# A new order of entries for the first two groups, and unused products at the end removed, in a blocked linear attention that feeds a leaky-ReLU MLP

## The chip, the cores and the metric

The kernel runs on one core of one Trainium2 chip. The metric is the device time of one execution in microseconds (us), as the median of several runs. The profile shows one execution of the program, taken by the hardware profiler; its times count from the span's start.

The engines are named as the profile names them: PE (TensorE, matrix products) with PEld (its weight loads), DVE (VectorE), ACT (ScalarE), POOL (GpSimd) and SP (SyncE, which issues the transfers). Each executes its own instructions, and semaphores order them across engines.

## The reference

Everything is float32 to the caller except the two weight matrices, which arrive as float64. The first part is lightning attention over blocks of 64 tokens with a running state, the second a two-layer MLP on the same 3072 tokens.

```python
B, H, S, D = 4, 8, 768, 64            # q, k, v; lam has one decay for each head
for b in range(S // 64):
    sl = slice(b * 64, (b + 1) * 64)
    intra = einsum('bhic,bhjc->bhij', qb, kb) * Dmask     # Dmask = lam ** (i - j), lower triangle
    intra = einsum('bhij,bhjd->bhid', intra, vb)
    inter = einsum('bhid,bhde->bhie', qb * lam_pow, kv_state)
    out[:, :, sl] = intra + inter
    kv_state = lam ** 64 * kv_state + einsum('bhsd,bhse->bhde', kb * rev_pow, vb)

x = out.transpose(0, 2, 1, 3).reshape(3072, 512)
h = x @ w_in                          # 512 x 2048
g = maximum(0.01 * h, h)
return g @ w_out                      # 2048 x 512
```

## The kernel before

**Tiling.** The tokens are 24 chunks of 128, six for each batch. Four chunks are a group of 512 tokens (`GC = 4`), so there are six groups, numbered 0 to 5. The hidden width of 2048 is cut into eight pieces of 256, p = 0 to 7, called weights here.

**Three products for one.** Each operand of a product is split into a high part `h`, a low part `l` and their mixture `m`, and each product is done three times, with `h`, `l` and `m`. So each weight has tiles `wh`, `wl`, `wm`, and the attention's output has `xh`, `xl`, `xm`.

**Attention of one chunk.** `load_kq` and `load_v` issue the transfers (L338, L388). `transposes` turns k and q on TensorE (L403), k into a bank of PSUM, q into `pt`. ScalarE copies both out (L414, L415). L419 scales k by the decay, and L423 scales q. `scores` makes the products of k and q, and of k and v, in `psc`; both use the helper at L313. VectorE masks the first (L452) and adds the second to the state (L457, L459); GpSimd decays the state (L462). `outputs` makes the output in `po`, also at L313, in three parts. Between the second and the third stands a tiny copy, `seen_po` (L491), on VectorE or ScalarE. ScalarE then writes `xh` (L507), and VectorE `xl` (L508) and `xm` (L510).

**Weights.** `w_in(p)` loads a weight in two halves as raw 64-bit words (L566) into one of three buffers, `raw0` to `raw2`, in turn. Each half is turned into float32 by three instructions on ScalarE (L578, L580, L582) and two on VectorE (L584, L585). Then `parts` makes `wh` on ScalarE (L591) or VectorE (L593), and `wl` (L596) and `wm` (L602) on VectorE.

**Units.** `up(g, p)` is the product of one group with one weight: 24 matmuls of 512 columns (two blocks of 128 of the weight's 256 columns; in each, four pieces of the depth for `h`, for `l` and for `m`). A block lies in one of three banks (`b10`, `b11`, `b2`). After `h` and `l` ScalarE scales the bank (L658); then `m` is added, ScalarE applies the leaky ReLU (L661), and the result is stored to DRAM (L664). `up` can also be given some of the group's four chunks: `("up", 1, 1, 0, 3)` is group 1, weight 1, chunks 0 to 2 of the group, with matmuls of 384 columns, and `("up", 1, 1, 3, 4)` the last chunk, with matmuls of 128. When all groups are through, `down` multiplies by `w_out` (L700), and each result is combined (L722, L729) and stored (L732).

**Order.** Nothing is issued as it is written. The entries of the list `seq` are turned into operations, each with an engine, a planned length and what it needs. `Plan.emit` gives every operation a planned start and emits all in that order, so each engine executes its instructions in the plan's order. In `seq`, `("a", c)` is a whole chunk alone, `("b", 4)` starts chunks 4 and 5, `("r", c)` is a round (the outputs of chunk c with the scores of chunk c+1 and the transposes of chunk c+2), `("wi", p)` loads and splits a weight, `("ls",)` and `("lt",)` load keys and queries in small blocks that are turned by VectorE (L374, L383). Behind the list, the entries for groups 2 to 5 and for `down` are appended by a loop.

**Fillers.** Where the plan's second pass expects TensorE to wait over 0.4 us, and until the bank `b10` has its first use, `plan.idle` puts in transposes of the identity that nothing reads, one for each 0.22 us. They are L266, `busy`. Eleven stand ahead of everything (`WARM`).

**Constants of the order.** `KT` names the bank for the k transposes of chunks 0 to 3, and `EARLY` the number of blocks for which that bank is left out of the turn. For chunks below `QS`, L423 is done by VectorE straight from `pt`, otherwise by GpSimd from ScalarE's copy. For chunks below `KM` the plan may give L419 to VectorE, otherwise it is GpSimd's. For chunks below `GOFIRST`, the products of k and q come ahead of those of k and v.

**The end.** Behind `plan.emit()` stand matmuls whose result nobody reads: 12 with half of the rows and 12 with a quarter (L802), and 8 of 64 columns (L809).

## Time and profile before

| | |
|---|---|
| three runs | 610.75, 611.75, 612.11 us; median 611.75 |
| span of the profiled execution | 610.3 us |
| mean granted clock of TensorE | 0.997 |
| products of units (L640), in all | 392 for each of `h`, `l`, `m`; 376 of them 512 columns wide, 8 of 384, 8 of 128 |
| fillers (L266) | 30 |
| first product of a unit | 30.41 us |
| transfers in the first 20 us | DMA engines 96% busy, 205 GB/s |
| L566, from issue to landing | 4.1 / 5.5 / 7.3 us (shortest, median, longest) |
| DVE and ACT from 40 to 60 us | 19.3 and 17.1 of 20 us busy |

A row of the profile's timeline has the start, the length, the engine, the line, what it writes and reads, the shape and the number of instructions in it. In brackets stands the idle time of the engine ahead of the row and what ended it. The lengths of TensorE's rows overlap: matmuls are pipelined, and one of 512 columns is listed with 0.39 us though the next starts 0.23 us later. So what a matmul costs is read from start to start.

### The profile page before, as it was taken

What the parts mean: (1) busy time and instruction counts of PE and PEld (TensorE: products, weight loads), DVE (VectorE), ACT (ScalarE), POOL (GpSimd) and SP (SyncE); (2) the same over time, 40 slices, a digit from 0 to 9 for tenths busy, and PEclk for the clock granted to TensorE, in tenths of its full rate; (3) what the DMA queues carried; (4) which work ended last, traced back from release to release, by engine and by line L of the source; (5) the groups of instructions that cost most, each with busy time, mean ns of one, the idle gap of its engine ahead of it and who ended that gap; (6) DMA issues with size and microseconds to landing.
All of it is one profiled execution on the core that took longest, in us unless ns stands there. A gap on an engine that the chain in (4) does not pass through costs nothing.

```text
span 610.3 us, 13012 instructions
## 1 busy us (share of the span) xinstructions
PE 601.9 (99%) x5426; PEld 497.6 (82%) x5426; DVE 313.2 (51%) x418; ACT 269.9 (44%) x430; POOL 86.6 (14%) x90
## 2 busy tenths in 40 slices
PE   7799999999999999999999999999999999999999
PEld 5688888888888878888788888888888888888887
DVE  5899764334243426326366755545454544636531
ACT  4678974444455646555577522222222313214111
POOL 2564412114133004104000000000000000000000
PEclk9899999999999999999999999999999999999999
DMA  9999775666889878886686843524333343333201
GB/s 201 236 261 263 215 204 126 175 154 176 192 212 245 212 222 219 212 242 212 233 302 219 278 155 103 173 69 139 137 104 134 111 136 111 132 104 126 82 1 69
DMA packets 147754, 105.18 MB, mean 172 GB/s; under 512 B 123632, under 2 KB 124400, under 8 KB 147696
## 3 DMA queue, kind: packets, MB, share of 16 engines
q1 hardware_dynamic: 147552, 104.36, 58.8%
q8 instruction: 42, 0.69, 0.5%
q14 instruction: 16, 0.13, 0.1%
q10 hardware_dynamic: 144, 0.00, 0.0%
HBM read 68.69 MB, written 35.65 MB: 171 GB/s over the span
## 4 chain that ended last, share of the span: by engine, by line
PE 95%; DMA 2%; ACT 1%; DVE 1%; issue 0%; SPq 0%; ACTq 0%
PE b L640 42%; PE b L700 18%; PE po L700 11%; PE psc L700 11%; PE po L313 4%; PE psc L313 4%; PE pt L700 4%; DMA g<-gs 1%; DMA att<-in_v_dram 1%; PE pt L403 1%; DMA att<-in_q_dram 1%; PE po L403 0%; PE psc L802 0%; ACT att L415 0%; PE b L266 0%
## 5 line engine op out<-in xcount | busy, mean ns | idle before, releaser
L682 ACT ACTIVATE xh<-att 128x1024 fp32r<-128x1024 f32 x48 | 50.8, 1060 | 149.1 <-PE b L700 133.6
L683 DVE SCALAR_TENSOR_TENSOR xl<-att,xh 128x1024 fp32r<-128x1024 f32 x48 | 58.7, 1223 | 97.5 <-ACT xh L682 97.5
L640 PE MATMUL b<-xm,wm 128*128 128x512 f32 (+2 forms) x392 | 104.5, 392 | 0.7 <-ACT b L658 0.7
L640 PE MATMUL b<-xh,wh 128*128 128x512 f32 (+2 forms) x392 | 103.2, 386 | 0.8 <-ACT xh L507 0.8
L640 PE MATMUL b<-xl,wl 128*128 128x512 f32 (+2 forms) x392 | 103.4, 387 | 0.0
L640 PEld LDWEIGHTS b<-xh,wh 128*128 128x128 f32 x392 | 72.9, 188 | 16.0 <-ACT xh L507 0.9
L640 PEld LDWEIGHTS b<-xl,wl 128*128 128x128 f32 x392 | 72.7, 188 | 15.1 <-DVE wl L596 0.3
L640 PEld LDWEIGHTS b<-xm,wm 128*128 128x128 f32 x392 | 71.4, 188 | 16.0 <-ACT b L658 1.1
L658 ACT ACTIVATE b<-b 128x512 f32<-128x512 f32 (+2 forms) x97 | 56.1, 580 | 60.6 <-PE b L640 60.5
L661 ACT ACTIVATE gs<-b 128x512 f32<-128x512 f32 (+2 forms) x97 | 57.0, 592 | 44.2 <-PE b L640 38.3
L700 PE MATMUL b<-wh,xh 128*128 128x512 f32 x192 | 74.7, 389 | 0.0
L700 PE MATMUL b<-wl,xl 128*128 128x512 f32 x192 | 74.7, 389 | 0.0
L685 DVE SCALAR_TENSOR_TENSOR xm<-xl,xh 128x1024 fp32r<-128x1024 f32 x48 | 58.7, 1225 | 4.7
L462 POOL TENSOR_TENSOR att<-att 128x256 f32<-128x256 f32 x40 | 34.4, 861 | 58.7 <-DVE att L459 58.7
L700 PEld LDWEIGHTS b<-wh,xh 128*128 128x128 f32 x192 | 36.1, 188 | 7.5
L700 PEld LDWEIGHTS b<-wl,xl 128*128 128x128 f32 x192 | 36.0, 188 | 7.5
L423 POOL TENSOR_TENSOR att<-att 128x512 f32<-128x512 f32 (+1 forms) x20 | 25.3, 1265 | 95.6 <-PE po L313 34.7
L452 DVE TENSOR_TENSOR att<-psc,att 128x512 f32<-128x512 f32 x24 | 16.5, 689 | 43.1 <-PE psc L313 43.1
L584 DVE TENSOR_SCALAR w<-w 128x512 int32<-128x512 int32 x32 | 19.6, 612 | 36.0 <-ACT w L578 35.9
L700 PE MATMUL psc<-wh,xh 128*128 128x512 f32 x96 | 37.3, 389 | 0.0
L700 PE MATMUL psc<-wl,xl 128*128 128x512 f32 x96 | 37.3, 389 | 0.0
L700 PE MATMUL psc<-wm,xm 128*128 128x512 f32 x96 | 37.3, 389 | 0.0
(79 smaller groups left out, 810.4 us busy)
## 6 DMA issues: line engine op xcount, KB each, us to landing
att<-g SPq DMA_DIRECT2D x48, 512.0 KB, 3.3
g<-gs SPq DMA_DIRECT2D x47, 512.0 KB, 4.0
raw<-in_moe_w_in_dram SPq DMA_DIRECT2D x16, 512.0 KB, 5.5
raw<-in_moe_w_out_dram SPq DMA_DIRECT2D x16, 512.0 KB, 4.8
att<-in_k_dram SPq DMA_DIRECT2D x48, 128.0 KB, 4.3
att<-in_v_dram SPq DMA_DIRECT2D x24, 256.0 KB, 4.5
out_dram<-gs SPq DMA_DIRECT2D x23, 256.0 KB, 2.1
wo<-w SPq DMA_DIRECT2D x8, 512.0 KB, 5.9
```

Source lines behind the costliest of these rows:

```text
L313: nc.tensor.matmul(dst[HALF[cols]], lhsT=lhsT[HALF[rows]], rhs=rhs[HALF[rows]], start=start, stop=True, skip_group_check=True)
L423: add(eng, us, lambda: e.tensor_tensor(o, x, _bc(pow_q, 2, 2)[:, :, m, :], op=ALU.mult), ["fq", dep], [f"qsT{i}"])
L452: add("DVE", 0.69, lambda: nc.vector.tensor_tensor(sc, psc[:, :, lower, :], decay, op=ALU.mult), ["psc", "fk"], ["sc"])
L462: add("POOL", 0.7, lambda new=new, j=j: nc.gpsimd.tensor_tensor(state[(j + 1) % 4], new, _bc(lam_c, 2, D), op=ALU.mult), [f"st{j % 4}", "f ...
L584: add("DVE", 0.42, lambda: nc.vector.tensor_scalar(d, d, 3, None, op0=ALU.logical_shift_left), [], [key])
L640: nc.tensor.matmul(dst, lhsT=w[z][:, kk * 2 * P + f * P:kk * 2 * P + (f + 1) * P], rhs=x[z][:, kk, toks], start=start and kk == 0, stop=kk ...
L658: add("ACT", ns, lambda b=b: nc.scalar.activation(out=b, in_=b, func=AF.Copy, bias=0.0, scale=S + 1.0), [], [kb], rank=-1.5)
L661: add("ACT", ns, lambda b=b, r=r: nc.scalar.activation(out=r, in_=b, func=AF.Prelu, bias=0.0, scale=1.0 / WS, alpha=0.01), [kb], [f"gs{jg} ...
L682: add("ACT", 1.05, lambda: nc.scalar.activation(out=h, in_=graw[j], func=AF.Copy, bias=0.0, scale=NEAR), reads, wr("h"))
L683: add("DVE", 1.25, lambda: nc.vector.scalar_tensor_tensor(l, graw[j], 1.0, h.bitcast(F32), op0=ALU.mult, op1=ALU.subtract), reads + [f"rh{ ...
L685: add("DVE", 1.25, lambda: nc.vector.scalar_tensor_tensor(m, l.bitcast(F32), -S, h.bitcast(F32), op0=ALU.mult, op1=ALU.add), [f"rh{j}", f" ...
L700: nc.tensor.matmul(acc[tb][z // 2][:, cols], lhsT=ring[j][z][:, f * T + tb * P:f * T + (tb + 1) * P], rhs=W[pp][z][:, f * d_model:(f + 1) ...
```

## The change

The list for the first two groups is another one. No unit is split in it any more, and weight 1 is loaded behind chunk 1 rather than behind chunk 3. Five constants differ. The products behind `plan.emit()` are gone.

```diff
-    KT, EARLY = "b11", 2
-    QS = 4
-    KM = 2
+    KT, EARLY = "b11", 1
+    QS = 6
+    KM = 0
...
-    GOFIRST = 3
+    GOFIRST = 2
...
-    seq = [("a", 0), ("a", 1), ("a", 2), ("a", 3), ("wi", 1), ("b", 4), ("r", 4), ("up", 0, 1), ("wi", 0), ("r", 5),
-           ("wi", 2), ("wi", 3), ("up", 0, 0), ("up", 0, 2), ("up", 0, 3), ("r", 6), ("up", 1, 1, 0, 3), ("r", 7),
-           ("wi", 4), ("up", 0, 4), ("wi", 7), ("up", 1, 1, 3, 4), ("up", 1, 3), ("up", 0, 7), ("up", 1, 2),
-           ("wi", 6), ("up", 0, 6), ("wi", 5), ("ls",), ("up", 0, 5), ("r", 8), ("lt",), ("up", 1, 7), ("r", 9),
-           ("up", 1, 4), ("r", 10), ("up", 1, 0), ("r", 11), ("up", 1, 6), ("up", 1, 5)]
+    seq = [("a", 0), ("a", 1), ("wi", 1), ("a", 2), ("a", 3), ("wi", 0), ("b", 4), ("r", 4), ("wi", 4), ("up", 0, 1),
+           ("wi", 2), ("up", 0, 0), ("up", 0, 4), ("r", 5), ("r", 6), ("wi", 3), ("wi", 7), ("up", 0, 2),
+           ("up", 0, 3), ("wi", 6), ("r", 7), ("wi", 5), ("up", 0, 7), ("up", 1, 0), ("up", 1, 7), ("up", 1, 4),
+           ("up", 1, 5), ("up", 1, 6), ("up", 0, 6), ("ls",), ("lt",), ("up", 1, 2), ("up", 0, 5), ("r", 8),
+           ("r", 9), ("r", 10), ("up", 1, 3), ("up", 1, 1), ("r", 11)]
...
     plan.emit()
-
-    a, b = ring[0][0], W[0][0]
-    spare = acc[0] + acc[1]
-
-    def strips(n, times):
-        k = P // n
-        for _ in range(times):
-            for i in range(n):
-                r = slice(i * k, (i + 1) * k)
-                nc.tensor.matmul(spare[i], lhsT=a[r, 0:P], rhs=b[r, 0:T], start=True, stop=True, skip_group_check=True)
-
-    strips(2, 6)
-    strips(4, 3)
-    f = graw[0]
-    for _ in range(4):
-        for i in range(2):
-            nc.tensor.matmul(spare[2][HALF[i], 0:C2], lhsT=f[:, 0:C2], rhs=f[:, 0:C2], start=True, stop=True, skip_group_check=True)
```

In the built program this moves instructions on every engine up to the end of group 1; behind that, the order on TensorE is the same up to the removed products. TensorE has 1152 unit matmuls, all 512 columns wide, and 51 fillers; fourteen of them stand between the k and the q transposes of chunk 3. Ahead of the first product of a unit TensorE does the same scores and outputs, and the transposes of one half chunk fewer (q of chunk 5).

SP's order at the start is: k, q, v of chunk 0, k, q, v of chunk 1, both halves of weight 1, k, q, v of chunk 2, q and k of chunk 3, a half of weight 0, v of chunk 3, the other half of weight 0, k and q of chunk 4, both halves of weight 4, v of chunk 4. Before, it was: chunks 0 and 1, a half of weight 1, q and k of chunk 2, the other half of weight 1, v of chunk 2, q and k of chunk 3, q of chunk 4, v of chunk 3, a half of weight 0, k of chunk 4, q of chunk 5, v of chunk 4, the other half of weight 0.

ACT's order from the copy of chunk 3's k to the first product is now: L580 L578 L582 of weight 0's first half, L578 of its second half, L415 of chunk 3, L580 and L582 of the second half, L507 of chunk 2, L580 of weight 4, L415 of chunk 4, L582 of weight 4, L491 and L507 of chunk 3. Before, it was: L491, L507 of chunk 2, L415, L591 of weight 1, L580 and L582 of weight 0's first half, L491, L415, L507 of chunk 3, and only then L578 for both halves.

DVE's order there is now: L508 and L510 of chunk 1, L596 and L602 of weight 1, L423 and L452 of chunk 2, L459, L423 of chunk 3, L584 of weight 0, L491, L459, L585, L584, L508 of chunk 2, L452 of chunk 3.

## The prediction

> **What bounds the kernel now.** I read the page first. Its busy row and its chain of waits agree: TensorE works 99% of the span, and the end is a chain of its products.

> ```profile
> span 610.3 us, 13012 instructions
> PE 601.9 (99%) x5426; PEld 497.6 (82%) x5426; DVE 313.2 (51%) x418; ACT 269.9 (44%) x430; POOL 86.6 (14%) x90
> PEclk9899999999999999999999999999999999999999
> ```

> So time is only won where TensorE idles, runs at a lower clock, or does work that can go. The list of who TensorE waited for puts the longest waits at the start: 1.8 us for the values of chunk 3, 1.6 for VectorE's L459, 1.4 for the identity. Second view, TensorE in order of time before the first product of a unit (columns: start, length, what ran, and idle time before it):

> ```profile
> 24.43 1.57 PE L313 MATMUL psc<-att 64*64 64x64 f32 x64 [1.79 <-DMA att<-in_v_dram]
> 27.19 1.46 PE L313 MATMUL po<-att 64*64 64x64 f32 x48
> 28.58 0.66 PE L403 MATMUL pt<-att 128*128 128x128 f32 x4
> 29.16 0.46 PE L313 MATMUL po<-att 64*64 64x64 f32 x16
> 30.41 0.97 PE L640 MATMUL b<-xh,wh 128*128 128x512 f32 x3 [0.78 <-ACT xh L507]
> ```

> The first product starts at 30.41. From there on TensorE's idle time is one wait of 0.68 us at 224. So **the time is the moment of the first product, plus a fixed amount of product work, plus the tail**. Third, the clock, in stretches of 3.4 us (columns: stretch, length, busy time of each engine, granted clock, DMA share, GB/s):

> ```profile
> 21.57:24.98 3.41, 1.60 (x58) 1.32 (x60) 2.34 (x4) 2.20 (x3) 3.41 (x4) 1.00 1.02 279
> 24.98:28.40 3.42, 3.42 (x92) 2.97 (x87) 2.35 (x4) 1.41 (x2) 1.04 (x2) 0.50 0.80 178
> 28.40:31.80 3.40, 2.62 (x42) 2.02 (x35) 3.37 (x5) 2.69 (x6) 1.87 (x1) 1.00 1.04 266
> ```

> After a stretch with 1.60 of 3.41 us busy (47%) the next ran at half clock; after 2.62 of 3.40 it did not. Fourth, ScalarE before the first product:

> ```profile
> 25.84 0.79 ACT L580 ACTIVATE low<-raw 128x512 uint16<-128x512 uint32 x1 [1.45 <-DMA raw<-in_moe_w_in_dram]
> 28.72 0.16 ACT L491 COPY att<-po 128x2 f32<-128x2 f32 x1 [1.47 <-PE po L313]
> 29.27 0.59 ACT L415 COPY att<-pt 128x512 f32<-128x512 f32 x1 [0.39 <-PE pt L403]
> 29.75 0.60 ACT L507 ACTIVATE xh<-po 128x512 fp32r<-128x512 f32 x1
> ```

> ScalarE keeps its written order: at 25.84 it had stood 1.45 us for a weight. The conversions of the second half of weight 0 start at 30.24, behind the L507 of chunk 3, which releases the first product.

> **The change, part by part.** *The first product.* In the changed order SyncE issues raw, raw (weight 1) ahead of chunk 2; then k2, q2, v2, q3, k3, raw, v3, raw (weight 0), k4, q4, raw (weight 4). The set issued ahead of the third raw is the one issued before 17.96 in the old trace, so I start there, with the old slots:

> ```profile
> 17.96 1.01 SPq L338 DMA_DIRECT2D att<-in_q_dram  x2
> 19.07 0.46 SPq L388 DMA_DIRECT2D att<-in_v_dram  x1
> 19.58 0.73 SPq L566 DMA_DIRECT2D raw<-in_moe_w_in_dram  x1
> 20.41 0.96 SPq L338 DMA_DIRECT2D att<-in_k_dram  x2
> 21.46 2.32 SPq L338 DMA_DIRECT2D att<-in_q_dram  x2
> ```

> Raw 0.73, v3 0.46, raw 0.73, k4 0.96, q4 2.32 and some 0.08 between issues: v3 goes out at 18.8 (19.07 before), the second raw at 19.3, weight 4's first half at 23.5. L566's own view gives 4.1, 5.5 and 7.3 us to landing (min, median, max), so weight 4 lands at 29.0 (27.6 to 30.8), weight 0 at 24.8.

> That matters because of ScalarE's new order: L578 of weight 0, L415 of q3, L580, L582, L507 of chunk 2, **L580 of weight 4**, L415 of q4, L582, L491 and L507 of chunk 3. Two weights now stand ahead of what releases the first product. Queued behind that L580 is L491, for which TensorE's last part of chunk 3's output waits. From 29.0: L580 0.65 to the next start (13.23 to 13.88 in the old trace), L415 0.48 (29.27 to 29.75), L582 0.65: L491 at 30.8. From L491 to the first product took 30.41 - 28.72 = 1.69; chunk 5's q transposes (0.28 of them after L491's end) and their copy (0.15 of delay to L507) move away: 1.26. **First product at 32.0, so +1.6.** The second weight gives a floor: 24.8, plus 0.59, 0.48, 0.65, 0.65, 0.6 on ScalarE, 0.7 and 0.7 on VectorE (L508, L452) and 0.93 for the output products puts L491 at 30.1 anyway. With both landings at their minimum I get 30.6 (+0.2), with weight 4 at its maximum 33.8 (+3.4).

> *The clock.* In the last 4.5 us before 32.0 TensorE has the output products of chunk 3 (0.93 and 0.46) and nine fillers of L266, 0.11 each (the q transposes of the same shape take 0.66 for four with 0.33 of latency in it): 2.4 of 4.5, or 1.8 of 3.41. That lies between 1.60 (throttled) and 2.62 (not), nearer the first. I take a throttled stretch; all in products it costs half of 3.42, 1.7; some of it falls in the wait: **+1.2** (0 to 1.7).

> [...]

> *The moved transposes.* Chunk 5's q transposes now stand behind the first product: **+0.44**, four starts 0.11 apart (up to the row's 0.66).

> *Whole units.* Group 1's unit of weight 1 goes from 24 products of 384 columns and 24 of 128 to 24 of 512. TensorE's starts:

> ```profile
> 64.38 0.86 PE L640 MATMUL b<-xh,wh 128*128 128x384 f32 x4
> 65.08 0.85 PE L640 MATMUL b<-xl,wl 128*128 128x384 f32 x4
> ...
> 78.07 0.56 PE L640 MATMUL b<-xh,wh 128*128 128x128 f32 x4
> 78.47 0.61 PE L640 MATMUL b<-xl,wl 128*128 128x128 f32 x4
> ```

> Four of 384 take 0.69 from start to start, four of 128 take 0.40 to 0.44, and four of 512 take 0.91 (93.08 to 93.98 in the same view): 6 x 0.69 + 6 x 0.42 - 6 x 0.91 = 1.2. **-1.2**, all on TensorE's path.

> *The tail.* The last store is issued at 607.26 and lands 1.7 later (the median of L732's two half stores), at 609.0. The unused products run on until 609.39 and the program's end waits for them. Out: **-0.4** (0 if the end waits for something else, -0.45 at most).

> *Costed at nothing.* Fillers rise from 30 to 51; fourteen stand ahead of q3's transposes, which wait for `pt` anyway until VectorE's L423 of chunk 2, now behind both L596 and L602 of weight 1 (1.6 and 1.2 us). If that wait is gone they cost 14 x 0.11 = 1.5. Chunk 0's key scaling goes from VectorE (0.67) to GpSimd (1.06), idle for 8.07 us there; the q scalings of chunks 4 and 5 go from GpSimd (1.27, 1.93) to VectorE (0.69 each), covered because weight 1's and half of weight 0's parts are now made before the first product; uncovered, 1.4. Chunk 2's score order (keys by values first) waits for v2, in the same place in the data. The wait of 0.68 at 224 may go or double. Rounds 9 to 12 stand four or five groups of four products apart (0.91 each): the closest pair in the old order, 140.28 and 147.07, cost no idle time.

> Sum: +1.6 + 1.2 + 0.44 - 1.2 - 0.4 = **+1.6 us**. The profiled execution's 610.3 becomes 611.9; the median of the three runs, 611.75, lies 1.45 above its span, so the forecast is **613.4**.

> **The rivals.**
> 1. *The delay without the throttled stretch*: 1.6 - 1.2 = +0.4, 612.2. For it: more fillers, and 1.8 us is not 1.6. Against it: the wait is longer than the old one.
> 2. *The weights are in time* (the other side). If weight 0 lands by 23.2 and weight 4 by 25, ScalarE stands nowhere and values of chunk 3 set the start: 24.1 (0.3 sooner), then the old 6.0 to the first product, less 0.9 (products of 1.57 and 1.46 at the half clock take 1.16 and 0.93 elsewhere) and 0.43: 28.8 or so, -1.6. Sum -1.6 + 0.44 - 1.2 - 0.4 = -2.8, 609.0. It decides from a first product at 30.4 without a throttled stretch. For it: two weights of the old order landed 1.5 us apart. Against it: the median of 5.5 us.
> 3. *Weight 4 lands at its latest*: first product at 33.8, sum +3.4, 615.2. For it: one raw issue alone held SyncE for 2.70 us.
> 4. *The list starves products later*: weights 4, 7 and 5 are asked for sooner than in the old order. Against it: some 5 us of VectorE's work on weights 1 and 0 (L596, L602, L584, L585) is done before the first product instead of behind it. A starved unit would cost what rival 3 costs, and counts into its chance.

> **How the numbers follow.** This kernel can tell 0.2%, 1.2 us, from no change: 610.5 to 613.0. Forecast 0.47, rival 1 0.23, rival 2 0.15, rival 3 0.15. Rival 2 is faster; rival 1 is no change, with a little of the forecast (0.02); the rest is slower: 0.15, 0.25, 0.60. The range leaves out most of rival 2 and the far end of rival 3: 610.9 to 616.0; the forecast's own is 612.4 to 614.4.

> **What would show it.** Right: L580 or L578 idle for a weight of `moe_w_in` just ahead of L507 of chunk 2 or 3; a first L640 near 32; a stretch at 0.50 around it; no products of 384 or 128 columns; an end 0.9 us behind the last store's landing (1.3 before). Wrong: a first L640 before 30.4, or idle time of TensorE between 32 and 220.

## The result, and the profile after

The changed kernel took 613.45 us (median of 14 runs, 611.70 to 615.98), the kernel before 611.59 us beside it (14 runs, 610.73 to 612.14): a ratio of 1.0032 with a 95% interval of 1.0023 to 1.0040, so +1.4 to +2.4 us. In a second series it was 613.51 against 612.18 us, 1.0026 (1.0006 to 1.0047). It is slower by a little more than this measurement can tell, and the forecast of 613.4 us fits. The parts of its sum do not all fit.

The page and the chain of the profiled execution look like those of before:

```profile
span 609.9 us, 12908 instructions
PE 598.2 (98%) x5383; PEld 494.3 (81%) x5383; DVE 309.2 (51%) x417; ACT 270.9 (44%) x430; POOL 80.1 (13%) x89
PEclk9999999999999999999999999999999999999999
```

This execution has a shorter span than the profiled one of before (610.3), although the median is longer. All runs lie about 1.8 us above their span, so a median of 613.45 belongs to a span of 611.7: the profiled execution is the fastest of its 14. A single pair of profiles would have given the wrong sign. TensorE of the changed kernel ahead of the first unit product (start, length, what ran, idle time before it):

```profile
21.35 0.44 PE L403 MATMUL b<-att 128*128 128x128 f32 x2 [0.98 <-DMA att<-in_k_dram]
...
26.86 0.69 PE L313 MATMUL psc<-att 64*64 64x64 f32 x32 [0.82 <-ACT att L415]
...
29.93 0.93 PE L313 MATMUL po<-att 64*64 64x64 f32 x48 [1.25 <-DVE att L452]
...
32.32 0.96 PE L640 MATMUL b<-xh,wh 128*128 128x512 f32 x3 [0.24 <-ACT xh L507]
```

The first product starts at 32.32 in place of 30.41. No single wait is as long as the old 1.79; there are three of 0.82 to 1.25 us, each for something else: a DMA, ScalarE and VectorE. ScalarE, the same view:

```profile
25.66 0.67 ACT L578 ACTIVATE w<-raw 128x512 f32<-128x512 f32 x1 [0.75 <-DMA raw<-in_moe_w_in_dram]
26.24 0.57 ACT L415 COPY att<-pt 128x512 f32<-128x512 f32 x1
26.70 0.79 ACT L580 ACTIVATE low<-raw 128x512 uint16<-128x512 uint32 x1
27.36 0.76 ACT L582 ACTIVATE low<-raw 128x512 f16<-128x512 f32 x1
27.99 0.56 ACT L507 ACTIVATE xh<-po 128x512 fp32r<-128x512 f32 x1
28.74 0.78 ACT L580 ACTIVATE low<-raw 128x512 uint16<-128x512 uint32 x1 [0.18 <-DMA raw<-in_moe_w_in_dram]
...
30.93 0.16 ACT L491 COPY att<-po 128x2 f32<-128x2 f32 x1 [0.29 <-PE po L313]
31.67 0.60 ACT L507 ACTIVATE xh<-po 128x512 fp32r<-128x512 f32 x1 [0.58 <-PE po L313]
```

Both waits for a weight that were forecast are there: L578 of weight 0's second half at 25.66, and L580 of weight 4 at 28.74. But L491 waits last for TensorE's product in `po`, not for ScalarE's own queue. That product waited for L452, L452 stands on VectorE behind L508 of chunk 2, and L508 needs the L507 of 27.99. VectorE, the same view:

```profile
28.59 0.69 DVE L508 TENSOR_TENSOR xl<-po,xh 128x512 fp32r<-128x512 f32 x1 [1.79 <-ACT xh L507]
29.20 0.68 DVE L452 TENSOR_TENSOR att<-psc,att 128x512 f32<-128x512 f32 x1
```

So the wait that decides is the first of the two, for weight 0.

The clock in stretches of 3.4 us (stretch, length, busy time of PE, PEld, DVE, ACT and POOL, granted clock, DMA share, GB/s):

```profile
28.40:31.80 3.40, 2.13 (x70) 1.57 (x69) 3.21 (x6) 2.35 (x6) 0.94 (x1) 1.00 1.19 289
31.80:35.20 3.40, 3.16 (x18) 2.44 (x17) 3.37 (x6) 2.44 (x5) 1.26 (x2) 1.00 0.90 199
```

Ahead of the first product TensorE was busy for 2.13 of 3.40 us, and no stretch at half clock follows.

### The profile page after: what moved, and what is told of

It is laid out like the page before. It is cut to its first block, busy times and chain, and to the rows that moved or that the text cites. A ratio compares the mean times of both kernels' runs of the same rounds, so it can differ in the third digit from the quotient of the medians.

```text
span 609.9 us, 12908 instructions
## 1 busy us (share of the span) xinstructions
PE 598.2 (98%) x5383; PEld 494.3 (81%) x5383; DVE 309.2 (51%) x417; ACT 270.9 (44%) x430; POOL 80.1 (13%) x89
## 4 chain that ended last, share of the span: by engine, by line
PE 94%; DMA 2%; SPq 1%; ACT 1%; DVE 1%; issue 0%; POOL 0%; DVEq 0%; POOLq 0%
PE b L640 43%; PE b L700 18%; PE po L700 11%; PE psc L700 11%; PE po L313 4%; PE pt L700 4%; PE psc L313 3%; DMA att<-in_k_dram 1%; DMA raw<-in_moe_w_in_dram 1%; SPq L338 1%; PE po L403 0%; PE pt L403 0%; SPq L566 0%; SPq L388 0%; DVE w L585 0%
## 5 line engine op out<-in xcount | busy, mean ns | idle before, releaser
L640 PE MATMUL b<-xm,wm 128*128 128x512 f32 x384 | 103.1, 395 | 0.0
L640 PE MATMUL b<-xh,wh 128*128 128x512 f32 x384 | 102.2, 390 | 0.4 <-ACT xh L507 0.2
L640 PE MATMUL b<-xl,wl 128*128 128x512 f32 x384 | 102.4, 390 | 0.0
L640 PEld LDWEIGHTS b<-xh,wh 128*128 128x128 f32 x384 | 71.9, 188 | 16.2 <-ACT wh L591 0.6
L640 PEld LDWEIGHTS b<-xl,wl 128*128 128x128 f32 x384 | 71.8, 188 | 15.0
L640 PEld LDWEIGHTS b<-xm,wm 128*128 128x128 f32 x384 | 70.6, 188 | 15.2 <-ACT b L658 0.2
L658 ACT ACTIVATE b<-b 128x512 f32<-128x512 f32 x96 | 55.9, 584 | 57.8 <-PE b L640 57.6
L661 ACT ACTIVATE gs<-b 128x512 f32<-128x512 f32 x96 | 56.8, 597 | 43.6 <-PE b L640 38.6
L462 POOL TENSOR_TENSOR att<-att 128x256 f32<-128x256 f32 x40 | 30.4, 761 | 89.3 <-DVE att L459 88.3
L700 PE MATMUL po<-wh,xh 128*128 128x512 f32 x96 | 37.3, 389 | 0.0
L700 PE MATMUL po<-wl,xl 128*128 128x512 f32 x96 | 37.3, 389 | 0.0
L700 PE MATMUL po<-wm,xm 128*128 128x512 f32 x96 | 37.3, 389 | 0.0
```

Source lines behind the costliest of these rows:

```text
L462: add("POOL", 0.7, lambda new=new, j=j: nc.gpsimd.tensor_tensor(state[(j + 1) % 4], new, _bc(lam_c, 2, D), op=ALU.mult), [f"st{j % 4}", "f ...
L640: nc.tensor.matmul(dst, lhsT=w[z][:, kk * 2 * P + f * P:kk * 2 * P + (f + 1) * P], rhs=x[z][:, kk, toks], start=start and kk == 0, stop=kk ...
L658: add("ACT", ns, lambda b=b: nc.scalar.activation(out=b, in_=b, func=AF.Copy, bias=0.0, scale=S + 1.0), [], [kb], rank=-1.5)
L661: add("ACT", ns, lambda b=b, r=r: nc.scalar.activation(out=r, in_=b, func=AF.Prelu, bias=0.0, scale=1.0 / WS, alpha=0.01), [kb], [f"gs{jg} ...
L700: nc.tensor.matmul(acc[tb][z // 2][:, cols], lhsT=ring[j][z][:, f * T + tb * P:f * T + (tb + 1) * P], rhs=W[pp][z][:, f * d_model:(f + 1) ...
```

## The experiments

**More profiles of both kernels.**

> The changed kernel once more, with a second profile. Theory (the time is the moment of the first product plus fixed product work plus the tail; most executions are 1.5 to 2 us longer than the profiled one because the half-clock stretch or a later landing falls into the start of most of them): a first L640 at 32 to 33 us; if the span is 611 us or more, a stretch at 0.50 near 32 or a first L640 1 us or more later than in the first profile. Rival (the loss of the longer executions is spread over the dense part): a first L640 at 32.3 as before, no half-clock stretch, and more idle time of TensorE between 35 and 600. Time 612.5 to 614 either way.

> The changed kernel for a third profile. Theory (an execution is longer by a later first product or the half-clock stretch): for a span of 611 or more, a first L640 past 33 us or a stretch at 0.50. Rival (stalls behind it): first L640 at 32.3 to 32.6, and from the first product to the last more than 574.5 us.

> The kernel before once more, for a second profile. Theory (the first profile's 30.41 holds a half-clock stretch that most executions do not have): first L640 at 28.5 to 29.3 and no stretch at 0.50 ahead of it. Rival: 30.41 is its usual start, 30.0 or later.

The moments below are read from the timeline of each execution. The third line is the kernel before without the unused products, which is the same up to its end.

| execution | first product | from there to the start of the last product | from there to the end | span |
|---|---|---|---|---|
| before, first profile | 30.41 | 575.60 | 4.28 | 610.3 |
| before, second profile | 29.04 | 576.25 | 4.27 | 609.6 |
| before, unused products out | 28.62 | 575.94 | 3.90 | 608.5 |
| changed, first profile | 32.32 | 573.62 | 3.97 | 609.9 |
| changed, second profile | 32.62 | 574.18 | 3.96 | 610.8 |
| changed, third profile | 32.94 | 574.60 | 3.97 | 611.5 |

The theory held for the kernel before: without the half-clock stretch its first product comes at 28.6 to 29.0, and the 30.41 of the forecast held that stretch. For the changed kernel neither the theory nor the rival held alone. Its longer executions begin up to 0.62 later and lose up to 0.98 more behind that, 0.5 to 0.6 of which, from start to start, is the wait for L658 near 225 (absent in the first profile). None of its three profiles has the stretch. Taking three executions of each kernel, with 28.83 as the start of before (the mean of its two without the stretch): **+3.8 at the start, -1.8 to the last product, -0.3 at the end, +1.7 in all**, which lies within the interval of the medians. The agreement is a loose one. With the 30.41 counted into the start of before, the sum would be +1.2, and all three profiled executions of the changed kernel lie below the span of 611.7 that belongs to its median, so its longer executions are not taken apart here. Part of the earlier start of before is also lost again at once: in both executions without the stretch TensorE waits 0.53 us for L508 behind its first eight products.

**The unused products alone.** The kernel before, with everything behind `plan.emit()` taken out.

```diff
     plan.emit()
-    strips(2, 6)
-    strips(4, 3)
...
```

> The kernel before without the unused products behind the plan. Theory: 0.4 us faster, the end of the span 0.9 us behind the last store's landing. Rival (the program's end waits for something else): 0 to 0.1.

610.87 against 612.18 us, ratio 0.9982 (0.9967 to 0.9996): 0.2 to 2.0 us faster. In the table the end shrinks from 4.28 to 3.90. So the theory's 0.4 holds by the profile (the medians cannot tell it from 2.0), and this is the only version measured that is faster than both kernels.

**The whole unit alone.** The kernel before, with one entry less in the list.

```diff
-("up", 0, 3), ("r", 6), ("up", 1, 1, 0, 3), ("r", 7),
-("wi", 4), ("up", 0, 4), ("wi", 7), ("up", 1, 1, 3, 4), ("up", 1, 3),
+("up", 0, 3), ("r", 6), ("r", 7),
+("wi", 4), ("up", 0, 4), ("wi", 7), ("up", 1, 1), ("up", 1, 3),
```

> The kernel before with group 1's unit of weight 1 whole, at the place of its second part. Theory (a product of 384 or 128 columns costs more per column): 24 products of 512 in place of 24 of 384 and 24 of 128, 1.2 us faster. Rival (TensorE needs the first part to fill a wait that is there now): a wait of about 1 us appears near 65 us and the gain is 0 to 0.3.

613.09 us, ratio 1.0012 (0.9999 to 1.0025). The list of who TensorE waited for:

```profile
PE b L640 <- ACT wh L591: 1.7, 1, 1.7
...
PE b L640 <- DVE wl L596: 0.6, 1, 0.6
```

The wait of 1.7 stands near 64, where the split unit's first part had been: the rival held, and of its gain of 0 to 0.3 nothing is seen. The wait of 0.6 stands near 47, where all engines still have the order of before, so it is not the edit's doing. The split part bridged the time until the next weight was ready: taking it out wins 1.2 us of product work and opens a wait that is longer than that. The start-to-start times of L640 add up to 269.5 us, in place of 268.6 to 268.7 before. In the changed list, which orders the weights differently, no such wait stands and the gain stays.

**The conversions moved, first try.** The plan was told that weight 0's second half and weight 4 need `xh` of chunk 3.

```diff
+        late = ["xh03"] if kind == "wi" and (p, h) in LATE_HALVES else []
...
-            [f"raw{j}"], [key])
+            [f"raw{j}"] + late, [key])
```

> ScalarE's conversions of weight 0's second half and of weight 4 stand behind L507 of chunk 3, the rest as in the changed kernel. Theory (these conversions, waiting for their weights, hold L491 and L507 back): no L580 or L578 with idle time for a weight ahead of L507 of chunk 3, first unit product at 29.5 to 30.8 in place of 32.3, and the time 1.5 to 2.5 us below the changed kernel's. Rival (the values of chunk 3 or VectorE set the start anyway): first unit product not before 31.8, time within 0.6 us of the changed kernel's. Second rival (the earlier start is given back, because weight 0 and weight 4 are ready later): first product near 30, but waits of 1 us or more for wh, wl or wm behind it, time within 0.6 us.

630.56 us, 1.0287 (1.0257 to 1.0318), with waits of 8.2 us for values, the longest of 6.9 near 146 to 153. One new dependence made the planner change the orders of other engines too, SP's from 32.8 us on. So the time of this run says nothing of the question. Its start says a little: with SP's order the same until then, and with fewer fillers, the first product came at 31.23. The runs below keep the planned order.

**The conversions moved, order kept.** The changed kernel's own order is issued as it was planned. Only the marked operations, and what depends on them (loads into the same buffers too), are held back until a named one has been issued. TensorE's order and its fillers stay as they were, in this run and in those that follow.

```diff
+    def waits(i):
+        return not plan.ops[i][2] <= gone or i in late and gate not in gone
+    for t, _, i, e in plan.timeline:
+        held.append((i, e))
...
+LATE_HALVES = ((0, 1), (4, 0), (4, 1))
```

The gate is the L507 of chunk 3. The other two runs name only `(0, 1)`, or only the two halves of weight 4.

> The changed kernel with its own order kept on every engine; only ScalarE's conversions of weight 0's second half and of weight 4 (and what must follow them) are issued behind L507 of chunk 3. In the run where the list was planned anew, the loads of the values moved too, so that it tells nothing. Theory (these conversions hold L507 of chunk 2, L491 and L507 of chunk 3): first unit product at 30.0 to 30.8 in place of 32.3 to 32.6, no new wait over 0.5 us for a part of weight 0, and the time 1.5 to 2.3 us below the changed kernel's, 611.2 to 612.0. Rival (values, masks and VectorE's work set the start): first product not before 31.8, time 613 to 613.6. Second rival (given back by weight 0): first product near 30.3, then a wait of 1 us or more for wh, wl or wm between 34 and 45, time 612.5 to 613.6.

> The same with the conversions of weight 0's second half alone behind L507 of chunk 3; weight 4's L580 stays ahead of L491. As the prediction had it (weight 4 sets the moment, weight 0 is only a floor below it): the start hardly moves, first unit product 31.7 to 32.4, 0 to 0.6 us gained. Rival (weight 0's second half sets it, through L507 of chunk 2, L508 and L452 of chunk 3, and weight 4 does not matter): first product at 30.0 to 30.8, the whole gain of the run that moves both.

> The same with weight 4's conversions alone behind L507 of chunk 3. As the prediction had it (weight 4 sets the moment, weight 0's floor lies 0.7 below): first unit product at 31.3 to 31.7, 0.7 to 1 us gained. Rival (weight 0's second half sets it): no gain, first product at 32.2 to 32.6. If neither this run nor the one with weight 0 alone gains what the run with both does, two chains of almost one length end there.

Weight 4 alone: 614.23 us, 1.0028 (1.0013 to 1.0044), no gain. Here is how each first product stands to L578 of weight 0's second half, which starts when that half lands:

| execution | L578 starts | first product | between |
|---|---|---|---|
| changed, first profile | 25.66 | 32.32 | 6.66 |
| changed, second | 25.96 | 32.62 | 6.66 |
| changed, third | 26.28 | 32.94 | 6.66 |
| weight 4 moved away | 26.98 | 33.65 | 6.67 |

The distance is the same with weight 4's conversions ahead of L491 and without them: **weight 0's second half sets the start**. Weight 0 alone: 616.00 us, 1.0057 (1.0037 to 1.0076). The first product came at 32.61 all the same. ScalarE in that run:

```profile
25.99 0.60 ACT L507 ACTIVATE xh<-po 128x512 fp32r<-128x512 f32 x1 [0.42 <-PE po L313]
29.49 0.77 ACT L580 ACTIVATE low<-raw 128x512 uint16<-128x512 uint32 x1 [2.90 <-DMA raw<-in_moe_w_in_dram]
...
31.23 0.14 ACT L491 COPY att<-po 128x2 f32<-128x2 f32 x1
```

L507 of chunk 2 moved forward by 2 us, and then ScalarE stood 2.90 us for weight 4. This chain takes 32.61 - 29.49 = 3.12 from its landing. With L580 of weight 4 at 28.74, 29.30 and 29.64 in the three profiles of the changed kernel it would give 31.86, 32.42 and 32.76: 0.5 to 0.2 sooner than weight 0's chain does. So two chains of almost one length end there, as the expectation for weight 4 alone had it.

With both moved: 613.92 us, 1.0028 (1.0017 to 1.0039), within half a microsecond of the changed kernel. TensorE in that run:

```profile
28.02 0.84 PE L403 MATMUL pt<-att 128*128 128x128 f32 x4 [0.63 <-DMA att<-in_q_dram]
...
31.72 2.11 PE L640 MATMUL b<-xh,wh 128*128 128x512 f32 x8 [0.24 <-ACT xh L507]
35.63 0.55 PE L403 MATMUL po<-att 128*128 128x128 f32 x3 [1.80 <-DVE xl L508]
```

A third chain, the queries of chunk 4 (whose transposes stand ahead of the outputs of chunk 3), now holds the start at 31.72. So do five fillers behind those transposes: the outputs follow them at 29.33 without a wait, though the L452 that they need had ended at 28.3. In the changed kernel a wait of 1.25 stood there and the same fillers cost nothing. What was won is lost at 35.63: L508 of chunk 3 stands on VectorE behind the work on weight 0 that came later. The second rival's kind of loss came, at another operand than it named.

**VectorE's share moved too, then the loads, then L423.** Three further steps in the same manner. Each holds back (or pulls forward) what the run before had shown to wait.

```diff
-LATE_HALVES = ((0, 1), (4, 0), (4, 1))
+BEHIND = {("wi", 0, 1): (None, "xh03", "xh03", "xh03", "xm03", "xm03"),
...
-BEHIND = {("wi", 0, 1): (None, "xh03", "xh03", "xh03", "xm03", "xm03"),
+BEHIND = {("wi", 0, 0): (("q", 4), "xh03", "xh03", "xh03", "xm03", "xm03"), ("wi", 0, 1): (("q", 4), "xh03", "xh03", "xh03", "xm03", "xm03"),
+          ("wi", 4, 0): (("v", 4), "xh03", "xh03", "xh03"), ("wi", 4, 1): (("v", 4), "xh03", "xh03", "xh03")}
...
-BEHIND = {("wi", 0, 0): (("q", 4), "xh03", "xh03", "xh03", "xm03", "xm03"),
+BEHIND = {("wi", 0, 0): (("q", 4), "xh03", "xh03", "xh03", ("s", 4), ("s", 4)),
```

Each tuple says behind what the load, the three conversions on ScalarE and the two on VectorE are issued; `("s", 4)` is L423 of chunk 4, `"xm03"` the L510 of chunk 3.

> As the run with both weights' conversions behind L507 of chunk 3, and VectorE's share of weight 0's second half (L584, L585 and what follows) behind L508 and L510 of chunk 3 as well. Theory (the gain of the earlier start was given back because L508 stood behind that work on VectorE): no wait of TensorE for xl of 1.8 us, first product at 30.8 to 31.8, from the first to the last product 573.6 to 574.6, and a median of 612.0 to 612.8. Rival (the weight itself is late): the wait moves on to wh or wl of weight 0, 1 us or more between 36 and 42, and a median of 613 to 614.

> The same, and the loads of weight 0 moved behind q of chunk 4, those of weight 4 behind v of chunk 4, all conversions of both behind L507 of chunk 3; TensorE's order is the changed kernel's. Theory (two halves of a weight ahead of chunk 3's values and chunk 4's keys and queries set the start): first product at 28.6 to 29.6, as in the kernel before without the half-clock stretch, from the first to the last product 573.6 to 575, a median of 609.5 to 611, which is below both kernels. Rival (weight 0 is then late): first product as said, but 1.5 us or more of waits for parts of weight 0 or 4 between 34 and 50, a median of 611.5 to 613.

> As the run with the loads of weights 0 and 4 moved, and VectorE's L423 of chunk 4 (which frees pt for the next transposes) ahead of its work on weight 0. Theory (that run lost its earlier start to a wait of 3.1 us for this L423 and to half-clock stretches around its waits): no wait over 1 us for L423 of chunk 4, first product at 28.6 to 29.6 where no stretch at 0.50 lies ahead of it (about 3.4 later with two), median 611 to 613.5, 3.5 us or more below that run's 616.9. Rival (the weights are late behind it): the wait moves on to wh or wl of weight 0 or 4, 2 us or more before 60, median 615 or more. A median below 611 would beat both kernels.

VectorE's share: 614.61 us, 1.0058 (1.0032 to 1.0083). The wait of 1.80 is gone, and the start is 31.87, held by chunk 4's queries and the five fillers again. A new wait stands behind it:

```profile
28.12 0.89 PE L403 MATMUL pt<-att 128*128 128x128 f32 x4 [1.03 <-DMA att<-in_q_dram]
...
39.82 0.66 PE L403 MATMUL pt<-att 128*128 128x128 f32 x4 [2.00 <-DVE att L423]
```

The loads too: 616.94 us, 1.0087 (1.0062 to 1.0112). Two stretches at 0.52 and 0.50 lay ahead of its first product at 32.09, and the wait for L423 grew to 3.10. The fourteen fillers ran in these stretches, from 22.67 to 25.41, and the q transposes of chunk 3 followed without a wait, though the L423 that frees `pt` had ended at 22.7. So here fillers held the start, and the run does not test the loads by themselves. L423 first: 615.25 us, 1.0061 (1.0039 to 1.0083). TensorE and then ScalarE in this last run:

```profile
25.08 0.66 PE L403 MATMUL pt<-att 128*128 128x128 f32 x4 [2.61 <-DVE att L423]
...
31.82 2.13 PE L640 MATMUL b<-xh,wh 128*128 128x512 f32 x8 [0.24 <-ACT xh L507]
...
42.02 2.08 PE L640 MATMUL b<-xm,wm 128*128 128x512 f32 x4 [2.74 <-ACT b L658]
```

```profile
39.78 1.23 ACT L578 ACTIVATE w<-raw 128x512 f32<-128x512 f32 x2 [0.34 <-DVE wl L596]
...
41.36 0.60 ACT L658 ACTIVATE b<-b 128x512 f32<-128x512 f32 x1
```

With no weight and no query in the way, the start is still 31.82. Now it hangs on L423 of chunk 2, which frees `pt` at 25.08 and stands on VectorE behind the work on weight 1; one operation of that work, L596, took 2.11 us there, against 1.22 in the first profile of the changed kernel. And L658, which the units need, stands on ScalarE behind conversions of weight 4 that wait for VectorE's L596. All three missed their theory's median; the last has its rival's, by waits at other places than it named. No run that keeps the planned order brought the start below 31.7. None left out the fillers, so what the start would be without them is open.

## Why the prediction was right, point by point

- **The sum** (+1.6) agrees with the medians (+1.4 to +2.4) and with the profiles (+1.7). Its parts erred in both directions, and that the errors cancelled is luck.
- **First product, 32.0 (30.6 to 33.8)**: measured 32.32, 32.62 and 32.94. The moment was right, and weight 4 was forecast well: its first half took 5.1 to 5.3 us from issue to landing. The step that failed is that weight 4 sets the moment and weight 0 only gives a floor. The load of weight 0's second half was taken at the median of 5.5 us; it took 6.7 to 6.9 and landed at 25.6 to 26.3 instead of 24.8. So the floor became the setter, and its chain ends 0.2 to 0.5 later than weight 4's. That the number still came out is luck: the two chains happen to be of almost one length. In the way the text worked it out, the floor of 30.1 for L491 moves by the same 0.8 to 30.9, which is what the profile shows.
- **"So +1.6"** is the mis-sized term: it was taken against 30.41, a start that held a stretch at half clock. Against the 28.83 of executions without it the delay is +3.8.
- **The clock, +1.2**: none of the three profiles has the stretch. The estimate of 1.8 us busy was not far off: between the steps of the clock's records (last section) the three profiles have 2.15, 2.13 and 1.83 us in the last whole stretch before the first product. None was followed by half clock, so "nearer the first" was the wrong choice. A mean clock of 0.997 or less, as the first profile of before has, stands in 8 of 27 executions of the changed kernel and in 15 of 76 of the one before, of those whose clock was recorded. It adds to the spread of both and little to the difference. Together the two terms put the loss at +2.8 from 30.41; measured it is +2.2 from there, or +3.8 from 28.83. The delay was put too low by 2.2; the clock term, which did not come, made up for 1.2 of that, and the product work, -1.8 where the sum has +0.44 - 1.2, for the other 1.0.
- **Rival 1** (delay, no stretch, 612.2) had the right story for the clock and the wrong price, because its base was the same 30.41.
- **Whole units, -1.2**: no product of 384 or 128 columns is left, and L640's start-to-start times add up to 266.3 to 267.0 us instead of 268.6 to 268.7: -1.9, of which 1.2 would be the split, as forecast, and the rest fewer waits. The run with this part alone shows that the gain depends on the rest of the list.
- **Moved transposes, +0.44**: L403 takes 5.15 behind the first product, in place of 4.74 in the first profile of before: +0.41. The other two profiles of before have 5.71 and 5.01, with pauses between these transposes, so against them the term is not seen.
- **The tail, -0.4**: -0.3 in the table.
- **At nothing**: the fourteen fillers cost nothing where a wait stands behind them (1.45 us for L423 in the second profile, 1.35 in the third). In the first profile the keys of chunk 3 came late and the transposes followed the fillers at once, 0.2 us after `pt` came free. In the run with the loads moved they cost 2.7 us, at half clock, against the 1.5 that the forecast gave for that case. The wait near 224 for L658 varies between none and 0.6, and a new one of 0.32 stands near 72.
- **The median's distance to the span**, taken as 1.45, is 1.8 in every run: the profiled execution of before was its slowest of three.

What remains argued: that all the chains at the start go back to one cause, more weight data ahead of the chunks' data and more work on VectorE and ScalarE before 32 us. The runs show the chains one by one; no run removed them all. The five constants and the fillers were not changed alone either, so what each is worth stays open.

## What to carry to other kernels

Read a stall's price against several executions: the first product of before came at 30.41 in the one profile, with a half-clock stretch ahead of it, and at 28.62 and 29.04 in two others, and that difference is almost as large as the effect in question. Where a hand-made or planned order is dense, look for the second and third chain within a microsecond of the first before expecting a gain from undoing the first. Test single moves with the rest of the order pinned, since a planner that is run again answers another question.

## What the runs showed of the hardware

```profile
28.40:31.80 3.40, 1.31 (x65) 1.01 (x56) 0.86 (x2) 1.88 (x4) 1.54 (x2) 1.00 1.07 279
31.80:35.20 3.40, 3.28 (x17) 2.42 (x10) 1.16 (x3) 2.48 (x5) 0.00 (x0) 0.55 0.93 210
```

1.31 of 3.40 us busy, with a longest gap of 2.09, and the first products run at half clock (0.55 granted over the stretch; 0.43 from start to start instead of 0.227). The longest gap does not sort the cases: half clock followed this one of 2.09 and the 1.79 in the first profile of before, but neither the 2.00 ahead of 39.82 in the run with VectorE's share moved nor the 2.61 ahead of 25.08 in the run with L423 first.

The trace's clock records change in steps of 3.41 us (20.48, 3.41 and 583.68 long in the first profile of before), and their boundaries lie at different places: half clock begins at 24.98 there, at 32.1 with weight 0 alone moved and at 41.5 with L423 first. Between these boundaries, up to 600 us, the executions that have such records show the following stretches of 3.41 us at full clock. Of six with 1.6 us of work or less, five were followed by half clock (1.08 with the loads moved, 1.23 with L423 first, 1.32 with weight 0 alone moved, 1.36 in the first try with the conversions, 1.60 in the first profile of before) and one was not (1.48, with L423 first). Of 25 with 1.6 to 2.4 us, two were (1.72 in that first try, 2.36 with the loads moved). So in these executions the work between two boundaries sorts the stretches better than the longest gap does. The kernel before without its unused products is an example: its wait of 1.60, ahead of 23.97, crosses a boundary at 23.11, the stretches on both sides have 2.49 and 2.45 us of work, and no half clock follows. Nearly the same wait was followed by half clock in the first profile of before (1.79) and not in its second (1.70); that the place of the boundaries decides this is a guess, not shown. The 1.48, the 1.72 and the 2.36 remain unexplained.
